# Softmax attention and a Mish MLP on one core: k's maximum through DRAM, and a tail product one group later

## The chip, the cores and the metric

The kernel runs on one core of a Trainium2 chip. The metric is the device time of one execution in microseconds (us). An engine's own busy time is told with the engine's name: TensorE (PE; its weight loads are PEld), VectorE (DVE), ScalarE (ACT), GpSimd (POOL) and SyncE (SP), which here issues the DMAs.

## The reference

Linear attention over 8 batches, 8 heads, 576 rows and 64 columns, then an MLP over the 4608 rows of 512 columns that the heads make together:

```python
q_s = np.exp(q - np.max(q, axis=-1, keepdims=True))
q_s = q_s / (np.sum(q_s, axis=-1, keepdims=True) + 1e-09)
k_s = np.exp(k - np.max(k, axis=2, keepdims=True))      # over the 576 rows
k_s = k_s / (np.sum(k_s, axis=2, keepdims=True) + 1e-09)
kv = np.einsum('bhsd,bhse->bhde', k_s, v)
x = np.einsum('bhsd,bhde->bhse', q_s, kv)               # then to (4608, 512)
h = x @ w_in                                            # 512 -> 2048
g = h * np.tanh(softplus(h))                            # Mish
out = g @ w_out                                         # 2048 -> 512
```

The maximum of k is one number for each column of a head. It is taken over the rows, and that is the direction which the kernel's layout of k spreads over the partitions.

## The kernel before, in words

**Items and groups.** The attention is cut into 32 items, each two heads of one batch (128 columns together). The MLP is cut into 9 chunks of 512 rows: one for the first 512 rows of each batch, and a ninth for the 64 last rows of every batch, the tails. A chunk has 16 slots, one for each 128 columns of the hidden layer. A slot is 12 matmuls for `ph` (`h_mm`, line 406) and, three slots later, 12 matmuls for `po` (`out_mm`, line 429). Every product of float32 is made of three fp32r products of high and low parts. Four slots are a group (`group`, line 442); group n/4 also does the attention of item i = 4 + n/4, one item for the batch after the one whose MLP is running. Items 0 to 3, and the beginning of item 4, are done ahead of the groups by a written-out list (`PROLOGUE`), beside the loading and splitting of the weights.

**What a group does for attention.** The four slots are u = 0 to 3, and in each the order on TensorE is `h_mm`, the attention step, `out_mm`:

- u = 1: k times v (`a_kv`, `pkv`, 20 fp32 matmuls of 64 columns of weights), the denominators of q (`a_qscale`), the scaled block matrix `kvbd` and its high and low parts `kvr` (`a_kvs`), the load of the next v.
- u = 2: the transpose of q on VectorE (`a_qt`); behind `out_mm`, the maxima for the next item (`a_max`: `a_kmx` for k, `a_qm` for q), then the product of q with kv (`a_x`: three fp32r matmuls `px` over 512 rows and one fp32 product `pxt`, two records in the trace, over the tail of 64), and `a_split`, which copies `px` to the MLP's input and `pxt` to `xt_dram`.
- u = 3: `a_kmax1` for the next item in front of `out_mm`, and `a_kmax2` behind it.
- At the end: the exponentials of the next item (`a_exp`) and the loads of the one after (`a_load`).

**k's maximum.** k lies with 128 partitions of rows. `a_kmx` (line 210) reduces over the 5 rows that each partition has, on VectorE, to `kmx`, 128 partitions by 128 columns. `a_kmax1` transposes that on TensorE (`pk`, line 253) and VectorE reduces it (`mxd`, line 255) to one number for each partition, that is for each column. `a_kmax2` broadcasts and transposes it back on TensorE (`pb`, line 263), and VectorE subtracts `pb` from k (line 265). Then ScalarE takes the exponential, `ke` (line 277), which is the weights of `pkv`.

**What sets the order.** From the sixth group on (n = 20) the order on TensorE, ScalarE, VectorE and GpSimd is that of the code; SyncE's is the scheduler's. In the first five groups the scheduler orders all engines. The small PSUM tiles (`pkv`, `px`, `pxt`, `pk`, `pb`) share two buffers in turn (`ps_a`); `mxd`, `kmx` and `xt` have one buffer each. Items from 8 on (`COLS`) use an arrangement of q made by the host, `qs`, in which q's transpose is done by VectorE in 32 by 32 blocks; they are the 24 items which the change concerns. In every fourth group the four sums `po` of a chunk are copied out in u = 2 (`evac`, line 434), two by VectorE and two by ScalarE.

Of the kernel before, what the change touches and what calls it, by code (L numbers as in the profile page):

```python
# [8 lines left out]
F32 = mybir.dt.float32  # L9
# [3 lines left out]
ALU = mybir.AluOpType  # L13
AX = mybir.AxisListType
P = 128
# [7 lines left out]


@with_exitstack
def attn_mish_mlp(ctx: ExitStack, tc: tile.TileContext, q, k, v, w_in, w_out, qs, out):
# [15 lines left out]
    NITEM = B * HP  # L42
    START = 20
    COLS = 2 * HP
# [3 lines left out]
    cp = ctx.enter_context(tc.tile_pool(name="cp", bufs=1))  # L48
    lp = ctx.enter_context(tc.tile_pool(name="lp", bufs=1))
# [4 lines left out]
    pp = start.__enter__()  # L54
# [9 lines left out]
    for t in kvbd:  # L64
        nc.vector.memset(t, 0.0)

    cp.tile([P, 112], F32, tag="gap", name="gap0")
# [7 lines left out]
    def sub(eng, out, a, b):  # L75
        eng.tensor_tensor(out, a, b, ALU.subtract)  # L76
# [87 lines left out]

    at = {}
    xs = {}
    ap.tile([P, 40], F32, tag="gap", name="gap1")
    xt_dram = dp.tile([B, P, HP, ST], F32, name="xt_dram")

    vt = [p.tile([P, 2, NC + 1, D + 2], F32, tag=f"v{j}", name=f"v{j}") for j, p in enumerate((pp, pp, pp, lp))]  # L170

# [5 lines left out]
    def a_load(i):  # L177
        if i >= NITEM:
            return
        b, hp = divmod(i, HP)  # L180
        hs = slice(2 * hp, 2 * hp + 2)
        r = at[i] = {}
        if i >= COLS:
            t = r["q"] = lp.tile([P, NB, 32], F32, tag="q3", name=f"q{i}")
            nc.sync.dma_start(t, qs[i].rearrange("p (n f) -> p n f", f=32))
        for nm, src in (("k", k), ("q", q))[:1 if i >= COLS else 2]:
            t = (pp if i < 3 else lp).tile([P, 2, NC + 1, D], F32, tag=f"{nm}{min(i, 3)}", name=f"{nm}{i}")
            nc.sync.dma_start(t[:, :, 0:NC, :], src[b, hs, 0:SM, :].rearrange("h (p c) d -> p h c d", c=NC))
            tail = src[b, hs, SM:S, :].rearrange("h p d -> p h d")
            nc.sync.dma_start(t[0:ST, :, NC, :], tail)  # L190
            nc.sync.dma_start(t[ST:P, :, NC, :], tail)
            r[nm] = t
# [12 lines left out]
    def a_kmx(i):  # L205
        if i >= NITEM:
            return
        r = at[i]
        kmx = ap.tile([P, 2, D], F32, tag="kmx", name=f"kmx{i}")
        nc.vector.tensor_reduce(kmx, r["k"].rearrange("p h c d -> p h d c"), axis=AX.X, op=ALU.max)  # L210
        r["kmx"] = kmx
# [30 lines left out]
    def psum(i, tag, name):  # L242

        if i < HP and tag != "a":
            return (ps_h if tag == "h" else ps_o).tile([P, 512], F32, tag=tag, name=name)
        return ps_a.tile([P, 512], F32, tag="a", name=name)

    def a_kmax1(i):
        if i >= NITEM:
            return  # L250
        r = at[i]
        pk = ps_a.tile([P, 512], F32, tag="a", name=f"pk{i}")
        nc.tensor.transpose(pk[:, 0:P], r["kmx"].rearrange("p h d -> p (h d)"), ident)  # L253
        mxd = ap.tile([P, 1], F32, tag="mxd", name=f"mxd{i}")
        nc.vector.tensor_reduce(mxd, pk[:, 0:P], axis=AX.X, op=ALU.max)
        r["mxd"] = mxd

    def a_kmax2(i):
        if i >= NITEM:
            return  # L260
        r = at[i]
        pb = ps_a.tile([P, 512], F32, tag="a", name=f"pb{i}")
        nc.tensor.transpose(pb[:, 0:P], r["mxd"].to_broadcast([P, P]), ident)  # L263
        mb = pb[:, 0:P].rearrange("p (h d) -> p h d", h=2)
        nc.vector.tensor_tensor(r["k"], r["k"], mb.unsqueeze(2).to_broadcast([P, 2, NC + 1, D]), ALU.subtract)  # L265

    def a_exp(i, which="kq"):
# [59 lines left out]
    def a_qt(i):  # L327
        if i >= NITEM:
            return
        r = at[i]  # L330
        if i >= COLS:
            qT = ap.tile([P, S], F32, tag="ke", name=f"qT{i}")
            nc.vector.transpose(qT, r["qe"].rearrange("p n f -> p (n f)"))  # L333
            hi = ap.tile([P, SM], F32R, tag="qT", name=f"qTh{i}")
            nc.scalar.copy(hi, qT[:, 0:SM])  # L335
            lo = sp.tile([P, SM], F32R, tag="wc", name=f"qTl{i}")
            sub(nc.vector, lo, qT[:, 0:SM], hi.bitcast(F32))
            r["qTl"] = lo
            r["qT"] = hi, qT[:, SM:S]
            return  # L340
        pool = pp if i in (0, 2) else ap
        qT = pool.tile([P, SM], F32, tag="qT", name=f"qT{i}")
        qTt = pool.tile([P, ST], F32, tag="qTt", name=f"qTt{i}")
        pq = psum(i, "o1", f"pq{i}")
        for c in range(NC):
            nc.tensor.transpose(pq[:, c * P:(c + 1) * P], r["qe"][:, c].rearrange("p h d -> p (h d)"), ident)
        nc.scalar.copy(qT, pq)
        pq2 = psum(i, "o2", f"pqt{i}")
        nc.tensor.transpose(pq2[:, 0:P], r["qe"][:, NC].rearrange("p h d -> p (h d)"), ident)
        nc.scalar.copy(qTt, pq2[:, 0:ST])  # L350
        r["qT"] = qT, qTt

    def a_x(i):
        if i >= NITEM:
            return
        b, hp = divmod(i, HP)
        r = at[i]
        qT, qTt = r["qT"]
        px = psum(i, "o3", f"px{i}")
        if i >= COLS:  # L360
            nc.tensor.matmul(px, kvr[0], qT, start=True, stop=False)  # L361
            nc.tensor.matmul(px, kvr[1], qT, start=False, stop=False)  # L362
            nc.tensor.matmul(px, kvr[0], r["qTl"], start=False, stop=True)  # L363
        else:
            nc.tensor.matmul(px, kvbd[i in (1, 3) or i >= HP], qT, start=True, stop=True)
        px2 = psum(i, "a", f"pxt{i}")
        nc.tensor.matmul(px2[:, 0:ST], kvbd[i in (1, 3) or i >= HP], qTt, start=True, stop=True)  # L367
        r["px"] = px, px2

    def a_split(i):  # L370
        if i >= NITEM:
            return
        b, hp = divmod(i, HP)
        px, px2 = at.pop(i)["px"]
        split_x(i, px)
        xt = ap.tile([P, ST], F32, tag="xt", name=f"xt{i}")
        nc.scalar.copy(xt, px2[:, 0:ST])
# [64 lines left out]
    def group(n):  # L442
        i = HP + n // G
        for u in range(G):
            m, o = n + u, n + u - LAG
            if m < NSLOT:
                h_mm(m)
            if u == 0 and NITEM <= i < NITEM + HP:
                t_load(i - NITEM)
            elif u == 1:  # L450
                a_kv(i)
                a_qscale(i)
                a_kvs(i)
# [33 lines left out]
    with tc.manual_schedule(engines={ET.PE}):  # L487
        for token in PROLOGUE.split():
            name = token.rstrip("0123456789")
            if name == "C":  # L490
                first_units()
            else:
                stages[name](int(token[len(name):]))
        ap.tile([P, 104], F32, tag="gap2", name="gap2")
# [39 lines left out]
```

## Time and profile before

| | |
|---|---|
| three runs, us | 951.95, 952.63, 955.1 (median 952.63) |
| the profiled execution, us | 951.55 |
| its span, first to last instruction, us | 949.9 |
| PE busy, share of the span | 93% |
| DVE busy | 54% |
| ACT busy | 33% |
| POOL busy | 18% |
| mean granted TensorE clock | 0.976 |
| matmuls `ph` and `po`, records | 3456 |
| matmuls `pk`, `pb`, records | 32 and 32 |

A busy PE is not a PE at its peak, because matmuls overlap in its pipeline: the record of one 128x512 matmul is 389 ns long, while the next one starts some 227 ns later. So the cost of an instruction on TensorE is read from the chain of work that ended last, which shows for each piece the time that it alone adds, and not from the length of its record.

### The profile page before, as it was taken

What the parts mean: (1) busy time and instruction counts of PE and PEld (TensorE: products, weight loads), DVE (VectorE), ACT (ScalarE), POOL (GpSimd) and SP (SyncE); (2) the same over time, 40 slices, a digit from 0 to 9 for tenths busy, and PEclk for the clock granted to TensorE, in tenths of its full rate; (3) what the DMA queues carried; (4) which work ended last, traced back from release to release, by engine and by line L of the source; (5) the groups of instructions that cost most, each with busy time, mean ns of one, the idle gap of its engine ahead of it and who ended that gap; (6) DMA issues with size and microseconds to landing.
All of it is one profiled execution on the core that took longest, in us unless ns stands there. A gap on an engine that the chain in (4) does not pass through costs nothing.

```text
span 949.9 us, 11408 instructions
## 1 busy us (share of the span) xinstructions
PE 880.2 (93%) x4272; PEld 711.6 (75%) x4272; DVE 508.9 (54%) x1078; ACT 312.2 (33%) x480; POOL 169.5 (18%) x146
## 2 busy tenths in 40 slices
PE   3686869999999999999999999999999999999990
PEld 2465658888888888888888888888888888888880
DVE  5899987355556555655565556555655122212210
ACT  3674655423333333333333333332333121111110
POOL 4577775210001000100000000000000000000000
PEclk9998989999999999999999999999999999999995
DMA  6685431211121112111211112111210020010001
GB/s 169 205 273 173 127 106 41 85 29 41 41 85 41 41 41 84 41 41 41 73 53 41 41 55 71 41 41 41 85 41 2 14 71 7 0 45 1 1 0 45
DMA packets 88958, 58.67 MB, mean 62 GB/s; under 512 B 60744, under 2 KB 79176, under 8 KB 88904
## 3 DMA queue, kind: packets, MB, share of 16 engines
q1 hardware_dynamic: 88904, 57.96, 20.7%
q8 instruction: 33, 0.54, 0.2%
q14 instruction: 21, 0.17, 0.1%
HBM read 47.45 MB, written 10.49 MB: 61 GB/s over the span
## 4 chain that ended last, share of the span: by engine, by line
PE 84%; DVE 6%; POOL 2%; issue 2%; DMA 1%; ACT 1%; SPq 1%; ACTq 0%; POOLq 0%; DVEq 0%
PE po L429 40%; PE ph L406 39%; PE pkv L288 2%; DVE wc_out L116 1%; DVE wc_out L115 1%; DVE wc_in L115 1%; DVE raw_in L111 1%; DVE wc_in L116 1%; PE px L362 1%; PE px L361 1%; PE px L363 1%; DVE kmx L210 1%; PE pk L253 1%; DMA raw_out<-in_moe_w_out_dram 0%; PE pxt L367 0%
## 5 line engine op out<-in xcount | busy, mean ns | idle before, releaser
L406 PE MATMUL ph<-xs,wih 128*128 128x512 f32 x1152 | 365.5, 398 | 0.3 <-ACT xs L383 0.2
L429 PE MATMUL po<-wo,gh 128*128 128x512 f32 x1152 | 363.2, 396 | 0.0
L406 PEld LDWEIGHTS ph<-xs,wih 128*128 128x128 f32 x1152 | 214.1, 190 | 46.4 <-DVE xs L384 0.9
L429 PEld LDWEIGHTS po<-wo,gh 128*128 128x128 f32 x1152 | 213.4, 189 | 45.1
L406 PE MATMUL ph<-xs,wil 128*128 128x512 f32 x576 | 226.4, 393 | 1.2 <-POOL wil L76 1.2
L429 PE MATMUL po<-wo,gl 128*128 128x512 f32 x576 | 226.0, 392 | 0.0
L417 DVE CAST gh<-y 128x512 fp32r<-128x512 f32 x144 | 67.2, 467 | 291.5 <-ACT y L414 291.5
L414 ACT ACTIVATE y<-ph 128x512 f32<-128x512 f32 x144 | 86.1, 598 | 290.9 <-PE ph L406 279.0
L406 PEld LDWEIGHTS ph<-xs,wil 128*128 128x128 f32 x576 | 109.0, 189 | 25.4 <-POOL wil L76 1.6
L429 PEld LDWEIGHTS po<-wo,gl 128*128 128x128 f32 x576 | 108.9, 189 | 23.5
L76 DVE TENSOR_TENSOR gl<-y,gh 128x512 fp32r<-128x512 f32 x124 | 85.8, 692 | 7.8
L306 POOL TENSOR_TENSOR qe<-qe,qs 128x576 f32<-128x576 f32 (+1 forms) x32 | 38.6, 1207 | 279.1 <-ACT y L414 196.2
L76 POOL TENSOR_TENSOR q<-q,qm 128x576 f32<-128x576 f32 (+1 forms) x32 | 39.9, 1248 | 232.2 <-issue 210.2
L277 ACT ACT_TABLE_LOAD x31 | 39.8, 1283 | 81.9 <-DVE k L265 81.8
L210 DVE TENSOR_REDUCE kmx<-k 128x128 f32<-128x640 f32 x32 | 41.2, 1288 | 6.2 <-DMA k<-in_k_dram 6.2
L414 ACT ACT_TABLE_LOAD x34 | 43.6, 1283 | 0.6
L335 ACT CAST qTh<-qT 128x512 fp32r<-128x512 f32 x24 | 14.9, 621 | 84.1 <-DVE qT L333 82.8
L265 DVE TENSOR_TENSOR k<-k,pb 128x640 f32<-128x640 f32 x32 | 26.1, 816 | 24.9 <-PE pb L263 24.8
L383 ACT CAST xs<-px 128x512 fp32r<-128x512 f32 x32 | 18.8, 587 | 53.4 <-PE px L363 50.4
L76 POOL TENSOR_TENSOR gl<-y,gh 128x512 fp32r<-128x512 f32 x20 | 28.4, 1421 | 33.5 <-DVE gh L417 30.4
L253 PE MATMUL pk<-ident,kmx 128*128 128x128 f32 x32 | 9.7, 303 | 20.8 <-DVE kmx L210 15.0
L434 ACT COPY ob<-po 128x512 f32<-128x512 f32 x24 | 14.1, 587 | 43.0 <-PE po L429 41.4
(76 smaller groups left out, 655.3 us busy)
## 6 DMA issues: line engine op xcount, KB each, us to landing
out_dram<-ob SPq DMA_DIRECT2D x36, 256.0 KB, 2.1
k<-in_k_dram SPq DMA_DIRECT2D x32, 256.0 KB, 2.8
raw_in<-in_moe_w_in_dram SPq DMA_DIRECT2D x16, 512.0 KB, 4.8
v<-in_v_dram SPq DMA_DIRECT2D x64, 128.0 KB, 2.8
raw_out<-in_moe_w_out_dram SPq DMA_DIRECT2D x16, 512.0 KB, 5.5
q<-in_qs_dram SPq DMA_DIRECT2D x24, 288.0 KB, 3.0
k<-in_k_dram SPq DMA_DIRECT2D x64, 32.0 KB, 2.6
q<-in_q_dram SPq DMA_DIRECT2D x8, 256.0 KB, 3.0
```

The source lines that it names most:

```text
L76: eng.tensor_tensor(out, a, b, ALU.subtract)
L115: nc.vector.scalar_tensor_tensor(a, a, 3, low, ALU.logical_shift_left, ALU.bitwise_or)
L116: nc.vector.scalar_tensor_tensor(a, high, 0x80000000, a, ALU.bitwise_and, ALU.bitwise_or)
L210: nc.vector.tensor_reduce(kmx, r["k"].rearrange("p h c d -> p h d c"), axis=AX.X, op=ALU.max)
L253: nc.tensor.transpose(pk[:, 0:P], r["kmx"].rearrange("p h d -> p (h d)"), ident)
L265: nc.vector.tensor_tensor(r["k"], r["k"], mb.unsqueeze(2).to_broadcast([P, 2, NC + 1, D]), ALU.subtract)
L277: nc.scalar.activation(e.rearrange("p c h d -> p h c d"), r[nm], AF.Exp)
L306: nc.gpsimd.tensor_tensor(q2, q2, z.unsqueeze(2).to_broadcast([P, n, w]), ALU.mult)
L406: nc.tensor.matmul(ph, wi[a][:, t, fs], x[:, z], start=t == 0 and i == 0, stop=t == HP - 1 and i == 2)
L414: nc.scalar.activation(y, ph, AF.Mish)
L417: nc.vector.tensor_copy(hi, y)
L429: nc.tensor.matmul(po[t], g[a][:, t * P:(t + 1) * P], wo[f][:, z], start=f == 0 and i == 0, stop=f == NF - 1 and i == 2)
```

## The change

For items from 8 on, the host hands in a second arrangement of k, `kt`, with the 128 columns of an item on the partitions and its 576 rows along them. `a_load` loads it (288 KB). `a_kmx` reduces it on VectorE straight to `mxd`, writes those 128 numbers to a row of a DRAM buffer, and reads the row back into all partitions as `mb`. `a_kmax1` does nothing for these items, and `a_kmax2` subtracts `mb` from k, without a transpose. So two transposes on TensorE go, one reduction on VectorE goes and another has a new form, and three DMAs are added for each item.

The tail's product `pxt` of item i is no longer made behind `px` in u = 2. It is made in u = 1 of the next group, directly in front of k times v of the next item, and its copy and its DMA to `xt_dram` follow there. For that, q's transpose is made in two instructions, of 512 and of 64 columns, and the tail has a tile of its own, `qTt`. The last item's tail (31) falls in the group after the last item, which has no k times v. Some padding tiles (`gap`) change; and the transposed q of items 0 and 2 lies in the room of `kt`.

```diff
+            t = r["kt"] = lp.tile([P, S], F32, tag="kt", name=f"kt{i}")
+            nc.sync.dma_start(t, kt[i])
...
 def a_kmx(i):
...
+        if i >= COLS:
+            mxd = ap.tile([P, 1], F32, tag="mxd", name=f"mxd{i}")
+            nc.vector.tensor_reduce(mxd, r["kt"], axis=AX.X, op=ALU.max)
+            nc.sync.dma_start(mx_dram[i].rearrange("(p o) -> p o", o=1), mxd)
+            mb = r["mb"] = ap.tile([P, 2, D], F32, tag="kmx", name=f"mb{i}")
+            nc.sync.dma_start(mb.rearrange("p h d -> p (h d)"), mx_dram[i:i + 1, :].to_broadcast([P, P]))
+            return
...
     def a_kmax1(i):
-        if i >= NITEM:
+        if i >= COLS:
             return
...
-        pb = ps_a.tile([P, 512], F32, tag="a", name=f"pb{i}")
-        nc.tensor.transpose(pb[:, 0:P], r["mxd"].to_broadcast([P, P]), ident)
-        mb = pb[:, 0:P].rearrange("p (h d) -> p h d", h=2)
+        if i >= COLS:
+            mb = r["mb"]
+        else:
+            pb = ps_a.tile([P, 512], F32, tag="a", name=f"pb{i}")
+            nc.tensor.transpose(pb[:, 0:P], r["mxd"].to_broadcast([P, P]), ident)
+            mb = pb[:, 0:P].rearrange("p (h d) -> p h d", h=2)
         nc.vector.tensor_tensor(r["k"], r["k"], mb.unsqueeze(2).to_broadcast([P, 2, NC + 1, D]), ALU.subtract)
...
-            qT = ap.tile([P, S], F32, tag="ke", name=f"qT{i}")
-            nc.vector.transpose(qT, r["qe"].rearrange("p n f -> p (n f)"))
+            qe = r["qe"].rearrange("p n f -> p (n f)")
+            qT = ap.tile([P, SM], F32, tag="ke", name=f"qT{i}")
+            nc.vector.transpose(qT, qe[:, 0:SM])
             hi = ap.tile([P, SM], F32R, tag="qT", name=f"qTh{i}")
-            nc.scalar.copy(hi, qT[:, 0:SM])
+            nc.scalar.copy(hi, qT)
+            qTt = ap.tile([P, ST], F32, tag="qTt", name=f"qTt{i}")
+            nc.vector.transpose(qTt, qe[:, SM:S])
...
+        r["px"] = px
+        if i < COLS:
+            a_tail1(i)
+
+    def a_tail1(i):
+        r = at[i]
+        px2 = r["pxt"] = psum(i, "a", f"pxt{i}")
+        nc.tensor.matmul(px2[:, 0:ST], kvbd[i in (1, 3) or i >= HP], r["qT"][1], start=True, stop=True)
...
+        split_x(i, at[i]["px"])
+        if i < COLS:
+            a_tail2(i)
+
+    def a_tail2(i):
         b, hp = divmod(i, HP)
-        px, px2 = at.pop(i)["px"]
-        split_x(i, px)
+        px2 = at.pop(i)["pxt"]
         xt = ap.tile([P, ST], F32, tag="xt", name=f"xt{i}")
         nc.scalar.copy(xt, px2[:, 0:ST])
         nc.sync.dma_start(xt_dram[b, :, hp, :], xt)
...
             elif u == 1:
+                late = COLS < i <= NITEM
+                if late:
+                    a_tail1(i - 1)
                 a_kv(i)
+                if late:
+                    a_tail2(i - 1)
                 a_qscale(i)
```

More of the change, by code (lines that the diff above doesn't have):

```diff
@@ L25, in attn_mish_mlp @@
 @with_exitstack
-def attn_mish_mlp(ctx: ExitStack, tc: tile.TileContext, q, k, v, w_in, w_out, qs, out):
+def attn_mish_mlp(ctx: ExitStack, tc: tile.TileContext, q, k, v, w_in, w_out, qs, kt, out):
     nc = tc.nc
@@ L65, in attn_mish_mlp @@
         nc.vector.memset(t, 0.0)
-    cp.tile([P, 112], F32, tag="gap", name="gap0")
     kvr = [cp.tile([P, P], F32R, tag=f"kvr{x}", name=f"kvr{x}") for x in "hl"]
@@ L166, in attn_mish_mlp @@
     xs = {}
-    ap.tile([P, 40], F32, tag="gap", name="gap1")
+    ap.tile([P, 40], F32, tag="gap0", name="gap0")
     xt_dram = dp.tile([B, P, HP, ST], F32, name="xt_dram")
+    mx_dram = dp.tile([NITEM, P], F32, name="mx_dram")
     vt = [p.tile([P, 2, NC + 1, D + 2], F32, tag=f"v{j}", name=f"v{j}") for j, p in enumerate((pp, pp, pp, lp))]
@@ L331, in a_qt @@
         if i >= COLS:
-            qT = ap.tile([P, S], F32, tag="ke", name=f"qT{i}")
-            nc.vector.transpose(qT, r["qe"].rearrange("p n f -> p (n f)"))
+            qe = r["qe"].rearrange("p n f -> p (n f)")
+            qT = ap.tile([P, SM], F32, tag="ke", name=f"qT{i}")
+            nc.vector.transpose(qT, qe[:, 0:SM])
             hi = ap.tile([P, SM], F32R, tag="qT", name=f"qTh{i}")
-            nc.scalar.copy(hi, qT[:, 0:SM])
+            nc.scalar.copy(hi, qT)
+            qTt = ap.tile([P, ST], F32, tag="qTt", name=f"qTt{i}")
+            nc.vector.transpose(qTt, qe[:, SM:S])
             lo = sp.tile([P, SM], F32R, tag="wc", name=f"qTl{i}")
-            sub(nc.vector, lo, qT[:, 0:SM], hi.bitcast(F32))
+            sub(nc.vector, lo, qT, hi.bitcast(F32))
             r["qTl"] = lo
-            r["qT"] = hi, qT[:, SM:S]
+            r["qT"] = hi, qTt
             return
-        pool = pp if i in (0, 2) else ap
-        qT = pool.tile([P, SM], F32, tag="qT", name=f"qT{i}")
-        qTt = pool.tile([P, ST], F32, tag="qTt", name=f"qTt{i}")
+        if i in (0, 2):
+            t = lp.tile([P, S], F32, tag="kt", name=f"qT{i}")
+            qT, qTt = t[:, 0:SM], t[:, SM:S]
+        else:
+            qT = ap.tile([P, SM], F32, tag="qT", name=f"qT{i}")
+            qTt = ap.tile([P, ST], F32, tag="qTt", name=f"qTt{i}")
         pq = psum(i, "o1", f"pq{i}")
@@ L365, in a_x @@
             nc.tensor.matmul(px, kvbd[i in (1, 3) or i >= HP], qT, start=True, stop=True)
-        px2 = psum(i, "a", f"pxt{i}")
-        nc.tensor.matmul(px2[:, 0:ST], kvbd[i in (1, 3) or i >= HP], qTt, start=True, stop=True)
-        r["px"] = px, px2
+        r["px"] = px
[5 more added lines that the diff above has]
+        nc.tensor.matmul(px2[:, 0:ST], kvbd[i in (1, 3) or i >= HP], r["qT"][1], start=True, stop=True)
     def a_split(i):
@@ L493, in attn_mish_mlp @@
                 stages[name](int(token[len(name):]))
-        ap.tile([P, 104], F32, tag="gap2", name="gap2")
+        ap.tile([P, 36], F32, tag="gap", name="gap")
         w_until(-1)
@@ L527 @@
     args.append(nc.dram_tensor("in_qs_dram", a.shape, _mybir.dt.float32, kind="ExternalInput").ap())
+    a = _np.ascontiguousarray(inputs['k'].transpose(0, 1, 3, 2)).reshape(B * H // 2, 128, S)
+    arrays["in_kt_dram"] = a
+    args.append(nc.dram_tensor("in_kt_dram", a.shape, _mybir.dt.float32, kind="ExternalInput").ap())
     DM = inputs['moe_w_out'].shape[1]
```

## The prediction

> **What bounds the kernel now.** I read the page first (busy slices, then the shares of the chain that ended last), then that chain in order of time over one group, then VectorE's and ScalarE's timelines over the same group, for the slack of the steps that move.
>
> ```profile
> PE   3686869999999999999999999999999999999990
> ...
> PE 84%; DVE 6%; POOL 2%; issue 2%; DMA 1%; ACT 1%; SPq 1%; ACTq 0%; POOLq 0%; DVEq 0%
> ```
>
> The first row is TensorE's busy share in 40 slices of 23.7 us: gaps in the first seven slices, none after. The second is the chain: 84% of the span hangs on TensorE. So from about 165 us on a nanosecond taken off TensorE is a nanosecond off the run, and work on any other engine costs nothing until TensorE waits for it. The changed items, 8 to 31, lie in that part. Here is the chain over one of their groups (start, us that the piece adds, what):
>
> ```profile
> 401.45 0.23 PE px L361
> 401.68 0.23 PE px L362
> 401.90 0.23 PE px L363
> 402.13 0.17 PE pxt L367 x2
> 402.30 2.82 PE ph L406 x12
> 405.12 0.11 PE pk L253
> 405.23 2.77 PE po L429 x12
> 408.00 0.11 PE pb L263
> 408.11 2.77 PE ph L406 x12
> 410.87 2.72 PE po L429 x12
> 413.59 2.72 PE ph L406 x12
> 416.31 0.74 PE pkv L288 x20
> 417.05 2.92 PE po L429 x12
> 419.97 2.72 PE ph L406 x12
> 422.69 2.72 PE po L429 x12
> 425.41 0.23 PE px L361
> ```
>
> The group is 425.41 - 401.45 = 23.96 us and has no idle piece. Twelve matmuls take 2.72 where nothing stands before them. Behind a small fp32 product they take more: 2.82 behind `pxt`, 2.77 behind `pk` and `pb`, 2.92 behind `pkv`. So each insertion has two prices, its own piece and the slower twelve behind it:
>
> - `pxt`: 0.17 + 0.10 = 0.27
> - `pk`: 0.11 + 0.05 = 0.16; `pb` the same
> - `pkv`: 0.74 + 0.20 = 0.94
>
> Eight times 2.72, three `px` and these make 21.76 + 0.69 + 0.27 + 0.32 + 0.94 = 23.98, which is the group, so nothing is counted twice.
>
> ```profile
> L361 PE MATMUL px<-qTh,kvrh x24: 389/389/389, 185.2 to 737.4; 128*128 128x512 f32 x24
> ```
>
> There are 24 such items; from the first `px` to the last are 23 periods of (737.4 - 185.2)/23 = 24.01 us. The 0.05 above 23.96 comes from every fourth group, where a chunk's sums are copied out. The chain there, and VectorE's row:
>
> ```profile
> 284.84 0.05 issue
> 284.89 0.30 PE pk L253
> ```
>
> ```profile
> 283.45 1.28 DVE L210 TENSOR_REDUCE kmx<-k 128x128 f32<-128x640 f32 x1
> ```
>
> VectorE ends k's first maximum at 284.73, behind the two copies, and `pk` must wait for it: 0.05 + 0.30 in place of 0.11, 0.24 more. By the mean period this happens (24.01 - 23.96) x 23 / 0.24 = 5 times.
>
> **The change, part by part.**
>
> *The two transposes.* `pk` and `pb` leave TensorE for 24 items: 24 x 0.16 = 3.84 us each, 7.7 us together. The wait of every fourth group goes with `pk`, 5 x 0.24 = 1.2 us. I take it that the slow twelve behind them (2.77) go too, since twelve behind a plain twelve take 2.72; the case that they don't is a rival.
>
> The length of the transpose's own record is much more than its piece of the chain:
>
> ```profile
> L253 PE MATMUL pk<-ident,kmx x32: 270/270/475, 5.7 to 717.1; 128*128 128x128 f32 x32
> ```
>
> The Trainium skill, in "TensorE: Matmul & The Clock Gate", Part 4, gives a transpose about 275 ns within a kernel, most of it access latency. The record's 270 ns agrees as a length; if TensorE were held for it, two transposes would cost 24 x 0.54 = 13.0 us instead of 7.7. I take the chain's pieces, because with them the group closes to 0.02 us.
>
> *The tail in front of k times v.* Today `pxt` costs 0.27, of which 0.10 is the slower twelve behind it. In its new place, no `ph` or `po` follows it, but `pkv`, which pays for its own return (0.20) already. What is left is its own two products. No row shows an fp32 product of 128 columns in front of one of 64, so I bound it. Ten steps of `pkv` (its two heads are records side by side) take 0.74, 0.074 each with the latency of the whole in it; two would be 0.15. Below that, they could vanish in the turn to `pkv` (0); above, they could keep all of 0.27, if the turn to weights of 64 columns makes a pause of its own; and 0.1 more, the return that `pxt` has now, if it makes both. I take 0.12, just under the two steps, because the nearest row is `pkv`'s own pace. So 0.15 is saved per item. 23 items have a `pkv` behind their tail; the last one stands alone and keeps its 0.27. 23 x 0.15 = 3.45 us; the bounds are 23 x 0.27 = 6.2 us and 23 x -0.1 = -2.3 us.
>
> *The new path of the maximum.* It is off TensorE, and costs nothing as long as it arrives in time:
>
> ```profile
> 400.54 1.30 DVE L210 TENSOR_REDUCE kmx<-k 128x128 f32<-128x640 f32 x1
> 401.76 0.74 DVE L233 TENSOR_REDUCE qm<-q 128x18 f32<-128x576 f32 x1
> ...
> 406.25 0.69 DVE L76 TENSOR_TENSOR gl<-y,gh 128x512 fp32r<-128x512 f32 x1
> 408.14 0.82 DVE L265 TENSOR_TENSOR k<-k,pb 128x640 f32<-128x640 f32 x1 [1.20 <-PE pb L263]
> ```
>
> ```profile
> 410.33 0.74 ACT L277 ACTIVATE ke<-k 128x640 f32<-128x640 f32 x1
> ```
>
> The new `mxd` reduces 576 contiguous numbers as `qm` does, 0.74 at 400.54, so it ends at 401.28. The write and the read then go one after the other through SyncE; the nearest rows are the DMAs of 32 KB, with the median to landing last, and the issue on SyncE:
>
> ```profile
> k<-in_k_dram SPq DMA_DIRECT2D x64, 32.0 KB, 2.6
> xt_dram<-xt SPq DMA_DIRECT2D x32, 32.0 KB, 1.4
> ```
>
> ```profile
> DMA to landing us min/median/max: 1.4/1.5/6.1
> ```
>
> ```profile
> 411.66 0.33 SPq L185 DMA_DIRECT2D q<-in_qs_dram  x1
> ```
>
> Write 0.33 + 1.5, read 0.33 + 2.6: the row is back at 406.0. (The line of three numbers is that of `xt_dram`, both ways.) VectorE's subtraction stands behind `gl`, which ends at 406.94, so the DMA is not even what it waits for, and it starts 1.2 us earlier than today. The latest start that TensorE does not feel: today it is 408.14 and `ke` ends at 411.07, 2.93 later; `pkv` starts at 416.31, so 413.38. The round trip has 413.38 - 401.28 = 12.1 us and needs 4.8. If the subtraction waits, the next `gh` and `gl` on VectorE and, behind `ke`, the next `y` on ScalarE wait with it; behind the waiting read on SyncE are the loads for the item after, which today too wait for `ke`. The load of `kt` adds one issue of 0.33 and 288 KB, as q's own, for data needed a group later. VectorE saves the 1.30 - 0.74 of the reduction and the reduction of `pk`, all in idle time.
>
> *Moved copies.* The copy of the tail and its DMA go to u = 1. On ScalarE the copy stands in front of that slot's `y` and waits for `pxt`, which comes directly behind the `ph` that `y` waits for anyway. Its row, and the row of what comes next on ScalarE:
>
> ```profile
> 402.65 0.22 ACT L377 COPY xt<-pxt 128x64 f32<-128x64 f32 x1
> ...
> 420.45 0.62 ACT L335 CAST qTh<-qT 128x512 fp32r<-128x512 f32 x1 [3.50 <-DVE qT L333]
> ```
>
> ScalarE idles 3.50 before the cast of q, and the copy takes 0.22 of that. On SyncE the DMA to `xt_dram` moves past the exponentials' loads and up to those of v, one issue of 0.33, needed only by the ninth chunk. The split of q's transpose adds one start of a VectorE instruction; the product `px` that needs it is at 425.41, five us after that cast. All of this I cost at nothing; without that cover the copy alone would be 0.22 a group, 5 us in all.
>
> *Sum.* 3.84 + 3.84 + 1.2 + 3.45 = 12.3 us. The profiled execution took 951.55 (a span of 949.9 and 1.65 around it): 951.55 - 12.3 = 939.2. The median of the three runs is 952.63, 1.1 above it, so I forecast 952.63 - 12.3 = 940.3 us. 0.3% of the time, about what a measurement can tell from no change, is 2.9 us.
>
> **The rivals.**
>
> *The tail gains nothing.* The turn from 128 to 64 columns costs what the return to fp32r did. For it: `pkv` itself makes the twelve behind it slower by 0.20, the most of all insertions, so turns of that kind are dear. Against it: two turns become one. Then 3.84 + 3.84 + 1.2 = 8.9 us are left: 943.7.
>
> *The slow twelve are not the transposes'.* If 2.77 comes from something else in u = 3 and 0, only 0.11 goes per transpose, 24 x 0.10 = 2.4 less: 942.7. Against it: the second twelve after `pb` is back at 2.72, in the middle of the same kind of work.
>
> *Transposes hold TensorE for their whole record* (13.0 in place of 7.7): 935.0. Against it: the sum of the group.
>
> *Slower: the round trip through DRAM is late.* The write is 128 pieces of 4 bytes, a form that no row shows. If both landings take the longest that `xt_dram` had, 6.1, the row is back at 401.28 + 2 x 6.43 = 414.14, 0.76 after the latest start; times 24 that is 18.2 us, and the run takes 940.3 + 18.2 = 958.5. The point from which TensorE waits is a round trip of 12.1 us; the point from which the gain is used up is 12.1 + 12.3/24 = 12.6 us. Against it: the median of the same kind of write is 1.5, and the DMA queues are nearly empty in this stretch. The Trainium skill speaks for it: in "DMA: Bandwidth & Descriptors", Specifications, it says that a piece below 512 bytes makes the DMA engine read, modify and write. No run here shows that with its price.
>
> *The start moves.* The first groups are ordered by the scheduler, and their tiles change places. No instruction of items 0 to 7 goes or comes, so I give this no sign, and a microsecond or two in the range.
>
> **How the numbers follow.** Chances: the forecast 0.68, the tail for nothing 0.15, the slow twelve 0.08, the full record 0.03, the late round trip 0.04, a start moved by more than two microseconds 0.02. The likeliest gives 940.3. The range reaches down to the free tail (6.2 in place of 3.45, 937.5) and up to the tail that gains nothing (943.7), with the spread of the runs around their median (0.7 below; I take as much above, and one microsecond more for the start): 936.8 to 945.5. Faster by over 0.3% (below 949.8) are all cases but the late trip and part of the moved start: 0.94; the same 0.02; slower 0.04.
>
> **What would show it right or wrong.** In the chain of the changed kernel: no `pk` or `pb` after 170 us; the three twelves that were 2.82, 2.77 and 2.77 at 2.72; `pxt` ahead of `pkv`, the two pieces together near 0.86, the twelve behind at 2.92; a period of about 23.96 - 0.32 - 0.15 = 23.49, the same in every fourth group. On VectorE: the subtraction directly behind `gl`, not waiting for a DMA. I am wrong if the period stays above 23.6 (the tail or the slow twelve), if `pkv` waits for `ke` (the round trip), or if the first `px` of item 8 is far from 185 us (the start).

## The result, and the profile after

The changed kernel takes 1058.12 us (median of 4 runs, 1054.04 to 1060.73) beside 952.76 us for the kernel before: a ratio of 1.1098, 95% interval 1.1057 to 1.1138. I had forecast 940.3, and 958.5 for the case that the trip through DRAM is late. The profiled execution took 1054.04 us, with a span of 1052.3.

The page's chain of the changed kernel, by engine and by line:

```profile
PE 32%; DMA 27%; DVE 22%; ACT 9%; issue 5%; POOL 2%; SPq 1%; DVEq 0%; ACTq 0%; POOLq 0%
DMA mx_dram<-mxd 18%; PE po L456 17%; PE ph L433 13%; DMA mb<-mx_dram 9%; ACT L289 3%; DVE gl L75 2%; DVE k L277 2%; DVE gh L444 2%; ACT L441 2%; DVE mxd L213 2%; DVE qs L313 1%; ACT y L441 1%; DVE wc_out L115 1%; DVE sw L232 1%; ACT qe L286 1%
```

TensorE's 84% of the chain have become 32%. The two small DMAs of the new path hold 27%. The span grew by 1052.3 - 949.9 = 102.4 us, and the first `px` of the items from 8 on shows where. First and last start stand behind the duration:

```profile
L379 PE MATMUL px<-qTh,kvrh x24: 389/389/504, 195.3 to 840.1; 128*128 128x512 f32 x24
```

- Up to item 8: 185.2 before, 195.3 now, 10 us more.
- From item 8 to item 31: 552.2 before, 840.1 - 195.3 = 644.8 now, 92.6 us more. That is 28.0 a group in place of 24.0.
- After item 31: 949.9 - 737.4 = 212.5 before, 1052.3 - 840.1 = 212.2 now.

Now the chain in order of time, from one k's reduction to the next (the pieces left out are short issues, and the small steps of q's and kv's scaling):

```profile
418.00 0.76 DVE mxd L213
418.77 8.16 DMA mx_dram<-mxd
...
426.99 3.70 DMA mb<-mx_dram
...
430.72 0.84 DVE k L277
...
431.61 1.28 ACT L289
...
433.55 0.67 ACT qe L286
434.23 1.28 ACT L441
435.53 0.61 ACT y L441
...
436.16 0.44 DVE gh L444
...
436.69 0.69 DVE gl L75
437.38 0.68 DVE qs L313
...
442.30 0.63 DVE qT L346
...
442.95 0.63 ACT qTh L348
...
443.61 0.69 DVE qTl L75
...
445.35 0.76 DVE mxd L213
446.12 10.16 DMA mx_dram<-mxd
```

Two things are to be seen. The write of 128 numbers takes 8 to 10 us. And TensorE is not in the chain at all in this stretch: the chain runs in a ring, from the reduction through the write, the read and the subtraction (L277), then through what ScalarE and VectorE have in their queues behind the subtraction, to the next reduction. From the subtraction's start to the reduction's end it is 446.11 - 430.72 = 15.4 us. The trip, from the first reduction's end (418.00 + 0.76) to the subtraction, is 430.72 - 418.76 = 12.0 us. TensorE only follows. The same view one turn earlier, at `pkv`:

```profile
404.10 0.74 ACT ke L289
...
404.89 0.81 PE pkv L300 x20
405.69 4.55 PE po L456 x12
```

`pkv` waits for `ke` (2.08 us in TensorE's timeline), and the twelve matmuls behind it take 4.55 in place of 2.92. The granted clock is down there: it is 0.50 from 407 to 409 us 1.00 again from 410.24 to 416, and 0.93 on average from 400 to 424 us. In the kernel before it is 1.00 in every such stretch. The waits of the whole run (us in total, times, longest):

```profile
DVE k L277 <- DMA mb<-mx_dram: 184.1, 23, 9.2
PE pkv L300 <- ACT ke L289: 61.8, 22, 4.5
```

And the write's landing, from its own line (lowest, median, highest), and in the table of DMA issues the load of `kt`, which is issued directly behind it, and q's load of the same size:

```profile
DMA to landing us min/median/max: 8.0/8.4/10.2
```

```profile
q<-in_qs_dram SPq DMA_DIRECT2D x24, 288.0 KB, 3.0
kt<-in_kt_dram SPq DMA_DIRECT2D x24, 288.0 KB, 10.8
```

The 10 us ahead of item 8 are on VectorE, in the first groups, which the scheduler orders. It has put the reduction of item 9 ahead of the scaling of item 7's kv, and a subtraction that must wait ahead of item 8's sums of q:

```profile
160.67 0.75 DVE L213 TENSOR_REDUCE mxd<-kt 128x1 f32<-128x576 f32 x1 [8.67 <-DMA kt<-in_kt_dram]
...
177.46 0.82 DVE L277 TENSOR_TENSOR k<-k,mb 128x640 f32<-128x640 f32 x1 [12.47 <-DMA xt_dram<-xt]
```

VectorE is idle for 8.67 us until `kt` has landed, and for 12.47 in front of a subtraction (the DMA named there may not be the one waited for).

So the theory: the write is slow because of its 4-byte pieces, and its time goes into a ring that is closed by the order of VectorE's and ScalarE's queues. The rivals: the load of `kt` makes the write slow; any trip through DRAM is as long; TensorE waits for the trip alone, whatever is queued; the tail's move has part in it.

### The profile page after: what moved, and what is told of

Same layout as the page of the kernel before. It is cut to its first block, busy times and chain, and to the rows that moved or that the text cites. A ratio compares the mean times of both kernels' runs of the same rounds, so it can differ in the third digit from the quotient of the medians.

```text
span 1052.3 us, 11410 instructions
## 1 busy us (share of the span) xinstructions
PE 910.3 (87%) x4224; PEld 737.6 (70%) x4224; DVE 497.4 (47%) x1078; ACT 305.4 (29%) x478; POOL 170.6 (16%) x146
## 4 chain that ended last, share of the span: by engine, by line
PE 32%; DMA 27%; DVE 22%; ACT 9%; issue 5%; POOL 2%; SPq 1%; DVEq 0%; ACTq 0%; POOLq 0%
DMA mx_dram<-mxd 18%; PE po L456 17%; PE ph L433 13%; DMA mb<-mx_dram 9%; ACT L289 3%; DVE gl L75 2%; DVE k L277 2%; DVE gh L444 2%; ACT L441 2%; DVE mxd L213 2%; DVE qs L313 1%; ACT y L441 1%; DVE wc_out L115 1%; DVE sw L232 1%; ACT qe L286 1%
## 5 line engine op out<-in xcount | busy, mean ns | idle before, releaser
L456 PE MATMUL po<-wo,gh 128*128 128x512 f32 x1152 | 383.2, 416 | 0.0
L433 PE MATMUL ph<-xs,wih 128*128 128x512 f32 x1152 | 361.0, 394 | 0.7 <-DVE xs L411 0.4
L456 PEld LDWEIGHTS po<-wo,gh 128*128 128x128 f32 x1152 | 228.7, 201 | 49.8
L456 PE MATMUL po<-wo,gl 128*128 128x512 f32 x576 | 235.2, 408 | 0.0
L444 DVE CAST gh<-y 128x512 fp32r<-128x512 f32 x144 | 73.3, 510 | 258.4 <-ACT y L441 257.6
L456 PEld LDWEIGHTS po<-wo,gl 128*128 128x128 f32 x576 | 115.8, 201 | 25.9
L277 DVE TENSOR_TENSOR k<-k,mb 128x640 f32<-128x640 f32 x24 | 20.1, 838 | 196.5 <-DMA mb<-mx_dram 184.1
L300 PE MATMUL pkv<-v,ke 128*64 128x66 f32 x480 | 25.0, 267 | 61.8 <-ACT ke L289 61.8
L300 PEld LDWEIGHTS pkv<-v,ke 128*64 128x64 f32 x480 | 21.1, 173 | 65.2 <-ACT ke L289 64.8
L313 DVE TENSOR_REDUCE qs<-qe 128x18 f32<-128x576 f32 (+1 forms) x32 | 24.4, 763 | 3.5 <-ACT qe L289 2.7
## 6 DMA issues: line engine op xcount, KB each, us to landing
kt<-in_kt_dram SPq DMA_DIRECT2D x24, 288.0 KB, 10.8
```

Of the source, the lines that this page charges most:

```text
L300: nc.tensor.matmul(pkv[j * D:(j + 1) * D, 0:D + 2], r["ke"][:, c, j], r["v"][:, j, c, :], start=c == 0, stop=c == NC)
L313: nc.vector.tensor_reduce(z, q2, axis=AX.X, op=ALU.add)
L433: nc.tensor.matmul(ph, wi[a][:, t, fs], x[:, z], start=t == 0 and i == 0, stop=t == HP - 1 and i == 2)
L444: nc.vector.tensor_copy(hi, y)
L456: nc.tensor.matmul(po[t], g[a][:, t * P:(t + 1) * P], wo[f][:, z], start=f == 0 and i == 0, stop=f == NF - 1 and i == 2)
```

## The experiments

Twelve kernels were run. Ratios are to the kernel before, run on the same chip; `px` times are the starts of the matmul, as in the rows above.

### The tail alone

The kernel before, with `a_tail1` and `a_tail2` and q's transpose in two, as in the changed kernel; `pk` and `pb` stay.

```diff
             elif u == 1:
+                late = COLS < i <= NITEM
+                if late:
+                    a_tail1(i - 1)
                 a_kv(i)
+                if late:
+                    a_tail2(i - 1)
```

> The kernel before with the tail's product alone moved in front of k times v (and q's transpose in two); k's maximum stays as it was. My step: 23 x 0.15 = 3.45 us faster, some 949.3 beside 952.8, with pxt and pkv together near 0.86 in the chain. Rival (the turn from 128 to 64 columns costs what the return did): no change, pxt and pkv together near 1.0 and the twelve behind at 2.92. Second rival (the tail has part in the 105 us of the changed kernel): 960 or more.

Measured: 951.84 us, ratio 0.9983 (0.9974 to 0.9992). The chain:

```profile
403.31 2.72 PE ph L418 x12
...
417.22 0.17 PE pxt L376 x2
417.39 0.74 PE pkv L288 x20
418.13 2.95 PE po L441 x12
```

The twelve behind `px` are at 2.72, as I had it. But `pxt` keeps its 0.17, and the twelve behind `pkv` take 2.95: 0.17 + 0.74 + 0.23 = 1.14 for what was 0.27 + 0.94 = 1.21. So the move is worth 0.07 a plain group, half of my 0.15. In every fourth group the period is 24.37 in place of 24.20: there `pk` waits for `kmx` either way, and `pxt` no longer lies within that wait. The mean period is 23.98 for 24.01. The tail is no cause of the slowdown.

### The write in 4 pieces of 128 bytes

```diff
-            mxd = ap.tile([P, 1], F32, tag="mxd", name=f"mxd{i}")
-            nc.vector.tensor_reduce(mxd, r["kt"], axis=AX.X, op=ALU.max)
-            nc.sync.dma_start(mx_dram[i].rearrange("(p o) -> p o", o=1), mxd)
+            nc.vector.tensor_reduce(mxw[:, 0:1], r["kt"], axis=AX.X, op=ALU.max)
+            mxt = ap.tile([P, 32], F32, tag="mxt", name=f"mxt{i}")
+            nc.vector.transpose(mxt, mxw)
+            nc.sync.dma_start(mx_dram[i].rearrange("(a f) -> a f", f=32), mxt.rearrange("(a b) f -> a b f", b=32)[:, 0, :])
```

> The changed kernel, but the 128 maxima are turned on VectorE first (a 32x32 block transpose of a 128x32 tile), so that the write is 4 pieces of 128 bytes in place of 128 pieces of 4. The same bytes go, and the same read follows. Theory (the small pieces make the write slow, 8.2 us): the write lands in 2 to 3 us, the round trip is about 7, under what the loop through VectorE's queue allows, the period is near 23.6 and the time 945 to 955, most of what is left being the start (px of item 8 was 10 us late). Rival (any write to DRAM that is waited for takes this long there, or the load of kt in the same queue holds it up): the write still takes 8 us and the time stays near 1055.

Measured: 957.96 us, ratio 1.0039 (1.0023 to 1.0054). Of the 105 us, 100 go with this one edit: `px` of item 8 starts at 187.3, and every period is 24.05. The load of `kt` lands in 2.8 us, and the read, which waits for the write, is issued 2.4 us behind it, where the changed kernel had 8.2. SyncE's timeline:

```profile
404.02 0.33 SPq L190 DMA_DIRECT2D kt<-in_kt_dram  x1
404.45 0.55 SPq L218 DMA_DIRECT2D mx_dram<-mxt  x1
406.81 0.33 SPq L220 DMA_DIRECT2D mb<-mx_dram  x1
```

The scheduler has also changed their order: `kt` is issued in front of the write here, and behind it in the changed kernel. So this run alone does not tell whether one held the other up; the run with the forms of the write, below, does. And 958 is more than I expected. The chain has a surprise:

```profile
404.66 2.80 PE ph L437 x12
407.46 2.75 PE po L460 x12
...
413.01 2.77 PE po L460 x12
```

No twelve of this stretch is at 2.72. Nothing waits; TensorE's matmuls themselves come more slowly. Three runs below are about that.

### The early maximum

The changed kernel, the write as it is, the reduction and both DMAs 11 us earlier:

```diff
+            if u == 0 and COLS <= i + 1:
+                a_kmx(i + 1)
             if u == 2:
-                a_max(i + 1)
+                if i + 1 < COLS:
+                    a_kmx(i + 1)
+                a_qm(i + 1)
```

> The changed kernel, with the reduction of kt and the two DMAs for the next item in u = 0 instead of u = 2 (items from 8 on), 11 us earlier; the write stays as it is. Theory (the loop is reduction, write, read, subtraction, and then all that VectorE has queued behind the subtraction, before the next reduction; that loop is what bounds): the wait of the subtraction for mb (184 us in 23 times) goes, the period falls to about 23.5 and the time to 940 to 950, although the write still takes 8 us or more. Rival (TensorE itself is slowed by the tail, or by the traffic of kt): the period stays near 28.

Measured: 953.49 us, ratio 0.9995 (0.9983 to 1.0007). The write still takes 8.9 us in the median, but every period is 23.57:

```profile
411.96 2.72 PE ph L433 x12
414.68 2.72 PE po L456 x12
...
425.56 0.17 PE pxt L391 x2
425.72 0.73 PE pkv L300 x20
426.46 2.94 PE po L456 x12
```

The ring is open, and TensorE is what bounds again, with most of the gain that I had forecast for it (23.57 a group, for 23.49). What eats the gain is the start: `px` of item 8 is at 199.0, 13.8 us later than before.

### Forms of the write

The kernel before, with one DMA more for each item from 8 on, for which nobody waits. An item has 128 rows of 1, 16, 128, 16 and 128 floats in `pr[0]` to `pr[3]` and `pr[5]`; `row` is one partition of SBUF. Each form was made four times.

```diff
+            if i % 6 == 0:
+                nc.sync.dma_start(pr[0][i], mxd)
+            elif i % 6 == 1:
+                nc.sync.dma_start(pr[1][i, :, 0:1], mxd)
+            elif i % 6 == 2:
+                nc.sync.dma_start(pr[2][i, :, 0:1], mxd)
+            elif i % 6 == 3:
+                nc.sync.dma_start(pr[3][i], ident[:, 0:16])
+            elif i % 6 == 4:
+                nc.sync.dma_start(row, mxd)
+            else:
+                nc.sync.dma_start(pr[5][i], ident)
```

> The kernel before, with one DMA more for each of the items 8 to 31, which nobody waits for; six forms in turn: 128 pieces of 4 bytes, adjoining (as in the changed kernel); 4 bytes every 64; 4 bytes every 512; 128 adjoining pieces of 64 bytes; 128 pieces of 4 bytes to a row of one partition in SBUF; 128 pieces of 512 bytes. Theory (pieces of 4 bytes are slow because they share what memory rewrites as a whole): the adjoining 4 bytes take 8 us to land, those 512 apart and the 512-byte pieces 1.5 to 2. Rival (any 4-byte piece is slow): all three forms of 4 bytes in DRAM take 8. Second rival (the load of kt behind the write makes it slow; there is none here): the adjoining 4 bytes take 2.

Measured (median to landing): 4 bytes adjoining 9.0 us; 4 bytes every 64 bytes 1.4; 4 bytes every 512 bytes 1.4; 64-byte pieces adjoining 1.6; 4 bytes adjoining in a row of one SBUF partition 1.9; 512-byte pieces 1.8. The answers for the first two lines:

```profile
L270 SPq DMA_DIRECT2D pr<-mxd x4: 332/332/333, 264.4 to 702.6; - x4
...
DMA to landing us min/median/max: 8.7/9.0/9.3
```

```profile
L272 SPq DMA_DIRECT2D pr<-mxd x4: 326/330/333, 290.5 to 726.9; - x4
...
DMA to landing us min/median/max: 1.4/1.4/1.4
```

(The 64-byte and 512-byte pieces were all issued at 137 to 142 us, ahead of their groups; the forms of 4 bytes lie in their groups, between 167 and 727 us.) So not the 4 bytes are slow, but 4 bytes beside 4 bytes in DRAM. The Trainium skill's rule that I cited for the late trip ("DMA: Bandwidth & Descriptors", Specifications: under 512 bytes the engine reads, modifies and writes) makes no difference between the three forms of 4 bytes. The pieces 64 bytes apart land as fast as any, so the rule by itself does not give the price. That the adjoining pieces wait for each other because they share a unit of memory fits this, but what that unit is, and who makes them wait, no run shows. No load of `kt` is in this kernel, so the write is slow without it, and that rival falls.

The run also shows that the slow write holds up what is issued behind it. The next load of k on SyncE, issued 4 to 6 us behind the write, lands after 7.1 and 5.8 us where the write had adjoining pieces (the loads at 416.04 and 561.96 us), and after 2.7 to 2.8 behind the pieces that lie 64 or 512 bytes apart. In the changed kernel it was `kt` that stood behind the write, and in the first groups VectorE waited for it. (The kernel was executed once, in 965.1 us; its added row moves the MLP's tiles, see below.)

### Padding to 64 bytes

The write in 4 pieces, with 8 floats of padding, because its tiles had moved everything behind them by 96 bytes.

```diff
+        ap.tile([P, 8], F32, tag="gap", name="gap")
         w_until(-1)
```

> The run with 4 pieces of 128 bytes, with 32 bytes of padding more, so that the MLP's inputs and weights begin at a multiple of 64 bytes in each partition, as they do in the kernel before and in the changed one (in that run they began 32 bytes off). Theory (the start address sets the pace: twelve matmuls took 2.80 and 2.77 there, 2.72 in the other kernels): all plain twelves at 2.72, the period about 23.55 in place of 24.05, the time about 944 (px of item 8 at 187, 23 periods, and 212.5 to the end as before). Rival (the traffic of the wide write and of kt slows TensorE): 2.80 and 958 stay.

Measured: 955.11 us, ratio 1.0015 (1.0003 to 1.0026), a period of 23.94, `ph` still at 2.79 and 2.80. A multiple of 64 bytes is not it.

### The new path from item 10 on

```diff
+    KC = COLS + 2
...
-        if i >= COLS:
+        if i >= KC:
             mxd = ap.tile([P, 1], F32, tag="mxd", name=f"mxd{i}")
```

The same bound stands in `a_load`, `a_kmax1` and `a_kmax2`; items 8 and 9 use TensorE as before.

> The changed kernel, but items 8 and 9 find k's maximum in the old way, on TensorE, so that the new path begins only at item 10, whose steps lie in the groups with an order written by the code. Theory (the 10 us of the start come from the scheduler, which pulls the reductions of items 8 and 9 ahead of other VectorE work, where they wait for kt): px of item 8 is back near 186, the periods from item 10 on stay at about 28, and the time is near 1045. Rival (the start is late because tiles or the tail moved): px of item 8 stays at 195.

Measured: 1060.54 us, ratio 1.1120 (1.1104 to 1.1137). `px` of item 8 is back at 187.4, so the start's loss comes from the new path in the groups that the scheduler orders. The 21 periods from item 10 on average 29.0, more than the 28.4 of the same periods in the changed kernel; I had expected 28 and 1045. The trips are longer by that much: from the reduction's end to the subtraction they take 13.2 us on average, for 12.6 in the changed kernel from item 10 on. Why they are longer stays open.

### Both repairs

The same, with the reduction in u = 0 as in the early maximum (with `KC` for `COLS`).

> The same with the reduction and the two DMAs in u = 0, as in the run with the early maximum. Both repairs together: px of item 8 near 186, two periods of 23.9, 21 of 23.57, 212.5 to the end: 941 us of span, 943 us, 1% faster than before, with a write that still takes some 9 us. Rival (the start's loss in the run with the early maximum has another cause): near 953 again.

Measured: 943.03 us, ratio 0.9883 (0.9867 to 0.9900), `px` of item 8 at 186.9, then 23.88 once and 23.57 for all the others. With the start and the ring both mended, nothing is left of the loss of 105 us.

### The subtraction one slot later

The kernel with the new path from item 10 on, at its place in u = 2; what waits for `mb` goes behind the next group's first slot.

```diff
-            elif u == 3:
+            elif u == 3 and i + 1 < KC:
                 a_kmax2(i + 1)
-        a_exp(i + 1)
-        a_load(i + 2)
+            elif u == 0 and i >= KC:
+                a_kmax2(i)
+                a_exp(i)
+                a_load(i + 1)
+        if i + 1 < KC:
+            a_exp(i + 1)
+            a_load(i + 2)
```

> The kernel with the new path from item 10 on, the reduction and the DMAs at their place in u = 2, but the subtraction, the exponentials and the next loads moved behind the first slot of the next group, so that the VectorE and ScalarE work of that slot isn't queued behind the wait for mb. Theory (what is queued behind the waiting subtraction closes the loop and makes 28): with the queues free the next reduction is on time, only ke itself is late, by 1 to 2 us a group, and the period is 24.5 to 25.5, the time 965 to 985. Rival (TensorE waits for mb's own latency, whatever is queued): 28 or more, 1040 or more.

Measured: 1021.13 us, ratio 1.0703 (1.0667 to 1.0739); the 21 periods average 27.1 beside 29.0. VectorE's wait for `mb` falls from 195.9 to 69.4 us in total, TensorE's for `ke` only from 72.2 to 53.4. So the queue has part in it, as the theory says, but I had expected 25 and 965 to 985. The plain groups are at 24.6 to 27.9, five of them at 25.2 to 25.3; those in which a chunk is copied out are at 30.0 to 31.3. Without the blocked queue, the trip itself is still too long for `pkv`.

### The 4 pieces, with the MLP's tiles where they were

```diff
-            mxt = ap.tile([P, 32], F32, tag="mxt", name=f"mxt{i}")
+            mxt = ap.tile([P, 32], F32, tag="kmx", name=f"mxt{i}")
...
+        ap.tile([P, 4], F32, tag="gap", name="gap")
```

> The changed kernel with 4 pieces of 128 bytes once more, all at its place in u = 2, but with the added tiles put into room that was there, so that the MLP's tiles lie where they lie in the changed kernel. Theory (the place of the MLP's inputs beside its weights sets the pace: both began at the same remainder of 512 bytes in the kernels with 2.72, at remainders 96 and 128 apart in the two wide runs): all plain twelves at 2.72, the period 23.57, px of item 8 at 187, the time 943 to 944. Rival (the wide write or its traffic slows TensorE): ph twelves at 2.80, a period of 23.94, 955.

Measured: 942.57 us, ratio 0.9886 (0.9870 to 0.9903), every period 23.57, `px` of item 8 at 186.3:

```profile
404.73 2.72 PE ph L437 x12
407.45 2.72 PE po L460 x12
...
413.79 2.92 PE po L460 x12
```

This is the changed kernel with the form of the write mended (and `kt` issued in front of it, as in the other runs with 4 pieces): 116 us less, and 1.1% faster than the kernel before. The trips take 5.4 to 6.0 us from item 10 on. It is level with the run of both repairs; the other ten kernels are slower.

### The same kernel, 128 bytes further

The run with both repairs, and 32 floats more of padding.

```diff
-        ap.tile([P, 36], F32, tag="gap", name="gap")
+        ap.tile([P, 68], F32, tag="gap", name="gap")
```

> The kernel with both repairs (early maximum, new path from item 10 on), with 128 bytes of padding more ahead of the MLP's inputs and nothing else. Theory (placement): the twelves of ph go from 2.72 to about 2.80, also after the last item, the period from 23.57 to about 23.95, the time from 943 to 953 or more. Rival (placement does nothing): 943.

Measured: 955.80 us, ratio 1.0026 (1.0016 to 1.0035), beside 943.03 without the padding. The period is 23.95. The twelves are slow behind the attention too, where only the MLP runs:

```profile
799.95 2.80 PE ph L435 x12
802.74 2.76 PE po L458 x12
```

So the place of the tiles behind the padding is worth some 13 us. Those are the MLP's inputs, but also `wo`, `y`, `gh` and `gl`; the weights `wih` and `wil` stay. The two wide runs with 2.80 fit this: in the program's own addresses, the first input and `wih` begin at the same remainder of 512 bytes in all kernels with 2.72, and 96 or 128 bytes apart in those with 2.80. The twelves of `po` are slower too (2.76), though `gh` and `wo` keep their distance, so which of the moved tiles matters is not shown, nor whether 512 is the number.

### Both repairs, the tail at its old place

`a_tail1` and `a_tail2` directly in `a_x` and `a_split` again, for all items.

> The kernel with both repairs, but with the tail's product at its old place behind px. Theory (the tail's move saves what the chain of the run with the tail alone showed: 0.27 + 0.94 before, 0.17 + 0.74 + 0.23 after, 0.07 a group): period 23.64 in place of 23.57, 23 x 0.07 = 1.6 us slower than with the tail moved, 944.6 or 0.9905 of the kernel before. My step in the prediction (0.15 a group): 946.5. Rival (the move is worth nothing): 943.

Measured: 945.52 us, ratio 0.9916 (0.9901 to 0.9930), period 23.65. The tail's move is worth 23.65 - 23.57 = 0.08 a group, 1.8 us in 23 groups, and 2.5 us between the medians, which are of two chips.

### A trip of 10 us

The fast kernel with 4 pieces, and two copies from DRAM to DRAM between the write and the read, which then reads the second copy.

```diff
+            for m in (0, 1):
+                nc.sync.dma_start(mx_more[m + 1][i].rearrange("(a f) -> a f", f=32), mx_more[m][i].rearrange("(a f) -> a f", f=32))
```

> The fast kernel with 4 pieces of 128 bytes at the old addresses, with two copies from DRAM to DRAM between the write and the read, so that the time from the reduction's end to the subtraction grows from 5.85 to about 10 us. My prediction gave this trip 12.1 us before TensorE would wait, counted from TensorE's side alone: by it, plain groups stay at 23.57, and the time below 950. Theory (loop): trip + 15.4 us of VectorE and ScalarE work in a row, from the subtraction to the next reduction's end, as the chain of the changed kernel has it (27.3 with a trip of 12.0), so a trip of 10 gives 25.4 a group and some 985.

Measured: 985.49 us, ratio 1.0334 (1.0294 to 1.0374), (772.3 - 193.9)/23 = 25.1 a group from the first `px` to the last. The first three periods are still at 23.57; the 20 after them average 25.4, the number expected. One group's trip in the chain, from the reduction's end to the subtraction:

```profile
418.40 0.76 DVE mxw L216
419.18 0.21 DVE mxt L218
...
419.60 2.37 DMA mx_dram<-mxt
421.99 2.74 DMA mx_more<-mx_dram
...
424.79 1.77 DMA mx_more<-mx_more
426.58 2.83 DMA mb<-mx_more
...
429.49 0.84 DVE k L284
```

The trip is 429.49 - 419.16 = 10.3 us. From item 10 on they take 8.5 to 11.6, all under the 12.1 that I had allowed, and the kernel is 33 us slower than the kernel before and 43 slower than the same kernel with the short trip. This separates the two: counted from TensorE's side, such a trip should have cost nothing.

## Why the prediction was wrong, step by step

**The two transposes: right.** 23.96 - 23.65 = 0.31 a group, for 0.32 forecast, with the slow twelves behind them gone. The wait of `pk` in every fourth group is gone too: all periods are alike. The record's length of 270 ns was indeed no price.

**The tail: right in kind, the term mis-sized.** 0.08 for 0.15. I had given `pxt` 0.12 in its new place, from `pkv`'s pace; it has 0.17 there as before, and the twelve behind `pkv` pay up to 0.03 more. With this, the forecast of 12.3 us becomes 12.3 - 23 x 0.07 = 10.7; the two runs that mend the rest have ratios of 0.9883 and 0.9886, a gain of some 11 us of 953.

**The write: wrong, and dear only through the next step.** "Write 0.33 + 1.5": the nearest row was a write of 128 pieces of 256 bytes, and the price of adjoining 4-byte pieces is six times that. My upper end, the longest landing of that row, 6.1, was no bound for another form; it measured 8.0 to 10.2. I had named the form as one that no row shows, and then given it the median of a row that it isn't like, and a chance of 0.04. By the rest of my working this alone would have cost little: the trips from item 10 on took 12.0 to 13.5 us, 12.6 on average, and with 12.1 allowed that is 0.5 a group, 12 us in all.

**"The round trip has 413.38 - 401.28 = 12.1 us": wrong, the step that failed.** I had counted the slack from TensorE's side alone: when must the subtraction start, so that `ke` is there for `pkv`? In the next sentence I named what waits with the subtraction, the next `gh`, `gl` and `y`, and gave that no price. These stand ahead of the sums of q, kv's scaling and q's transpose, and those ahead of the next reduction, so the ring is trip + 15.4 (16.6 to 18.0 in the groups that copy a chunk out). It turns in 23.57 only with a trip under 23.57 - 15.4 = 8.2 us, not 12.1. From item 10 on, trips of 12.6 and a rest of 15.8 on average make the 28.4 of the changed kernel, and trips of 9.7 with a rest of 15.7 make the 25.4 of the last experiment. With the reduction moved ahead in the queue, the write still took 8.9 us and the period was 23.57. With my own worst case (two landings of 6.1, a trip of 12.9) the ring gives 28.3 in place of 23.5, and 24 x 4.8 = 115 us, where I had 18.2. The rival had the right place and the wrong price.

**The start: wrong.** "No instruction of items 0 to 7 goes or comes, so I give this no sign." But their place in VectorE's queue changed: the scheduler set reductions and subtractions that wait for a DMA ahead of them. It cost 10 us, and 13.8 with the early maximum. With the 4 pieces a subtraction still waits ahead of other work there (6.30 us, at 165 us), but `px` of item 8 is at 186.3, 1 us later than before. So the order alone did not make the loss; it took the slow write with it.

**Placement: not in the prediction.** The changed kernel moves the MLP's inputs and weights, but both to the same remainder; the experiments that did not lost some 12 to 15 us.

## What to carry to other kernels

A step that is moved off the engine that bounds has two dates to keep: when its result is due there, and how soon the in-order queue in which somebody waits for it comes round to the step again. Add up that ring (the wait, and all that is queued behind it up to the next start) and compare it with the period; it can be the tighter of the two: here it allowed a trip of 8.2 us, and the slack that the bound engine showed was 12.1. And before a DMA's price is taken from the nearest row, look at how its pieces lie at the destination: a transpose of 32 by 32 ahead of the write, 0.21 us on VectorE, was worth 116 us here.

## What the runs showed of the hardware

- A write of 128 pieces of 4 bytes that adjoin in DRAM lands after 9.0 us. The same pieces 64 bytes apart land after 1.4, and in a row of one SBUF partition after 1.9. A load of 256 KB that was issued 5.5 us behind the adjoining pieces landed after 5.8 and 7.1 us, in place of 2.7 to 2.8 behind the 4-byte pieces that lie apart; the 288 KB of `kt`, directly behind them in the changed kernel, after 10.8.
- Twelve matmuls of 128x512 for `ph` took 2.80 us in place of 2.72, and twelve for `po` 2.76, when the MLP's inputs and all tiles behind them lay 128 bytes further and the weights `wih` and `wil` stayed. "TensorE: Matmul & The Clock Gate" of the Trainium skill, Part 2, says that loading the next weights takes no read bandwidth from the matmul that runs. Whether that loading has part in this effect no run here shows; the effect of the shift is shown, its cause is not.
- Where TensorE waited, the matmuls behind the wait were often slow too. In the group shown, a wait of 2.08 us was followed by twelve of 4.55 in place of 2.92, with the granted clock at 0.50 for 2 us. In the 22 groups of items 10 to 31 of the changed kernel, waits of 0.8 to 4.5 us stood in front of `pkv`; in 16 of them the twelve behind it took 3.6 to 5.2 us, in 6 they took 2.8 to 2.9 (from their first start to the start of the next `ph`). On average the waits are 61.8/23 = 2.7 of the 4.5 us a group above 23.57, and the slow twelves behind `pkv` some 1.2; the rest was not followed up.
